# The first layer and the last step of a convolution filter as four 64-row, 64-column TensorE tiles

## The chip, the cores and the metric

The kernel runs on one core of a Trainium2 chip. The metric is the time of one execution on the device, in microseconds (us). The engines are named as in the profile: PE (TensorE; PEld are its weight loads), DVE (VectorE), ACT (ScalarE), POOL (GpSimd) and SP, whose queue issues most transfers.

## The reference

Two stages follow each other: a gated long convolution over each of four sequences, whose filter comes from a small two-layer network, and a soft mixture of eight experts over all 45,824 tokens. The change lies in the filter, the first lines:

```
h_mlp = np.maximum(pos_emb @ w1, 0.0) @ w2          # (11456, 64) @ (64, 64), then @ (64, 128)
window = np.exp(-0.01 * pos)[:, None]
h_filt = h_mlp * window
u = x * v
y = irfft(rfft(u, 2S) * rfft(h_filt, 2S))[:, :S]     # S = 11456, per channel
out = x * y                                          # then the mixture of experts
```

## The kernel before, in words

The transforms are done as matrix products over a two-step factorization with N1 = 111 and N2 = 197: a position is 111 j + r with j below J = 99 and r up to 55 in either direction, so R = 56 values of r. The 128 channels go in G = 8 groups of 16. All products are fp32; each stands in the trace as two matmul instructions, each with its own weight load.

The filter comes first. `hid_load` brings `pos_emb` in 14 tiles `pos` (four r each): partitions 0 to 63 hold the 64 features of the positions 111 j + r, partitions 64 to 127 those of 111 j - r. `w1s` is `w1` as a block-diagonal 128 x 128 table (made on the host by `_twice`), so that one product with the tile gives the 64 outputs of both directions side by side. The window's factor in r is `wins`; since it is positive it is put into the weights ahead of the ReLU: `w1r[:, r]` is `w1s` times one column of `wins`. `hid_scale` makes these, some one at a time on DVE or ACT (`scale_one`), the rest several at a time on POOL (`scale_many`).

`hid_step` handles 4, then five times 8, then 4, 4, 2 and 2 values of r: one product per r (L161), then ACT applies ReLU to the first half (`hb`, L164), and DVE, twice, forms the second half's ReLU plus and minus `hb` (L166) and writes the hidden tensor `hid`. `idle_products` are products of zeros (L125), eight at the start, three after the first step and four at the end.

Then `filter_first` (L207) and `filter_second` (L219) transform `hid` over j and r into `F`. Group 0 of the signal goes through its first transform (`first`, L185, four tiles of 64 x 64 at `tile_position` (0 or 64, 0 or 64)); DVE has by then made its inputs (`p1_sd`). Last, in 13 rounds, `filter_last` multiplies eight frequencies of `F` by `w2` (L229: two tiles, each of 64 rows and 111 columns of weights), ACT copies the result into `ring`, and `p2` (L356 and after) forms the spectrum products of the same eight frequencies on PE, DVE and POOL. The seven other groups, the inverse transforms and the experts follow.

The order on each engine is that of the program text: `inorder` records every instruction, and `hid_scale` runs three steps ahead of `hid_step`. SP issues `wins`, the `pos` tiles, then the signal's `x` and `v` tiles and the tables, in that order.

Of the kernel before, what the change touches and what calls it, by code (L numbers as in the profile page):

```python
# [11 lines left out]
F32 = mybir.dt.float32  # L12
F32R = mybir.dt.float32r
AF = mybir.ActivationFunctionType
ALU = mybir.AluOpType
# [4 lines left out]
N1, N2 = 111, 197  # L20
L = N1 * N2
J = 99
# [3 lines left out]
R = 56  # L26
RP = 64
FO = 64
# [20 lines left out]
@with_exitstack  # L49
def conv_gate_moe(ctx: ExitStack, tc: tile.TileContext, xf, vf, xi, xe, pos, w1, w2, win,  # L50
                  t1x, t1h, wt, t3, t4, phi, mw1, mw2, rep, out):
    nc = tc.nc
    dram = ctx.enter_context(tc.tile_pool(name="dram", bufs=1, space=bass.MemoryType.DRAM))
    hs = dram.tile([G - 1, HP, J, 2 * CG], F32, tag="hs", name="hs")
    scr = dram.tile([D * TOK], F32, tag="scr", name="scr")
    cp = ctx.enter_context(tc.tile_pool(name="cp", bufs=1))
    moe = Moe(tc, cp, scr, phi, mw1, mw2, rep, out)
    with ExitStack() as cctx:
        conv_part(cctx, tc, cp, moe, xf, vf, xi, xe, pos, w1, w2, win, t1x, t1h, wt, t3, t4, hs, scr)
    moe.run(ctx)  # L60


def conv_part(ctx, tc, cp, moe, xf, vf, xi, xe, pos, w1, w2, win, t1x, t1h, wt, t3, t4, hs, scr):
    nc = tc.nc
# [3 lines left out]
    psh = hid_ps.enter_context(tc.tile_pool(name="psh", bufs=4, space=bass.MemoryType.PSUM))  # L68
# [9 lines left out]
    Tall = cp.tile([128, (B + 1) * 2 * CG * J], F32, tag="T", name="T")  # L78
# [4 lines left out]
    inorder = tc.keep_in_program_order  # L83

    RB = 4
# [6 lines left out]
    hid = moe.E[:J, : 2 * RP * FO].rearrange("p (s r f) -> p s r f", s=2, r=RP)  # L92
    Tf = T.rearrange("p s b c k i -> p (s b c) k i")
    Th = Tall[:, : J * 2 * FO].rearrange("p (k x) -> p k x", k=J)
    F = moe.E[:, : J * N1].rearrange("p (k n) -> p k n", n=N1)
# [1 line left out]
    ring = moe.E[:, J * N1 : J * N1 + 2 * HK * 2 * D]  # L97
    ring = ring.rearrange("p (t g k x) -> p t g k x", t=2, g=G, k=HK)
    small = moe.E[:, J * N1 + 2 * HK * 2 * D :]
    w1s = small[:, : 2 * FO]  # L100
    w2s = small[:, 2 * FO : 2 * FO + D]
    wins = small[:, 2 * FO + D :][:, :R]
    tab1h = small[:J, 2 * FO + D + R :][:, : 4 * J]
    w1r = Tall[:, : R * 2 * FO].rearrange("p (r x) -> p r x", r=R)
    spare = [moe.E[:, 4 * C * R + PW * i :][:, :PW] for i in range(2)]

    def hid_load(i):
# [9 lines left out]
    HR = 8  # L117
    sizes = [RB] + [HR] * 5 + [RB, RB, 2, 2]
    steps = [(sum(sizes[:i]), n) for i, n in enumerate(sizes)]
    zero = hid[:, 0, R : R + 2].rearrange("p r f -> p (r f)")  # L120
# [3 lines left out]
        for _ in range(n):  # L124
            inorder(nc.tensor.matmul(t, lhsT=zero, rhs=zero, start=True, stop=True))  # L125

    def scale_one(eng, r):
        if eng is nc.scalar:
            inorder(eng.activation(w1r[:, r], w1s, AF.Copy, scale=wins[:, r : r + 1]))
        else:  # L130
            inorder(eng.tensor_scalar_mul(w1r[:, r], w1s, wins[:, r : r + 1]))

    def scale_many(r0, r1):
        inorder(nc.gpsimd.tensor_tensor(
            out=w1r[:, r0:r1], in0=w1s.unsqueeze(1).to_broadcast([128, r1 - r0, 2 * FO]), op=ALU.mult,
            in1=wins[:, r0:r1].unsqueeze(2).to_broadcast([128, r1 - r0, 2 * FO])))

    def hid_scale(i):
        r0, n = steps[i]
        if i == 0:  # L140
            for r in range(1, n):
                scale_one(nc.vector, r)
        elif i == 1:
            for r in range(r0, r0 + 4):
                scale_one(nc.scalar, r)
            scale_many(r0 + 4, r0 + n)
        else:
            if n == HR:
                for r in range(r0 + n - 2, r0 + n):
                    scale_one(nc.scalar, r)  # L150
                n -= 2
            if n == 2:
                scale_one(nc.scalar, r0 + 1)
                n = 1
            scale_many(r0, r0 + n)

    def hid_step(r0, n):
        ph = psh.tile([J, HR, 2, FO], F32, tag="ph", name=f"ph_{r0}")
        for k in range(n):
            r = r0 + k  # L160
            inorder(nc.tensor.matmul(ph[:, k].rearrange("p h f -> p (h f)"), lhsT=pts[r // RB][:, r % RB],  # L161
                                     rhs=w1r[:, r] if r else w1s, start=True, stop=True))
        hb = ld.tile([J, HR, FO], F32, tag="lv", name=f"hb_{r0}", bufs=2)
        inorder(nc.scalar.activation(hb[:, :n], ph[:, :n, 0], AF.Relu))  # L164
        for s, op in enumerate((ALU.add, ALU.subtract)):
            inorder(nc.vector.scalar_tensor_tensor(out=hid[:, s, r0 : r0 + n], in0=ph[:, :n, 1], scalar=0.0,  # L166
                                                   op0=ALU.max, op1=op, in1=hb[:, :n]))

    def banks(g, u, name, large):
# [7 lines left out]
    def first(g, u, sd, large=False):  # L177

        ps = [t[:, : 4 * J].rearrange("p (c s k) -> p c s k", c=2, s=2) for t in banks(g, u, "p1", large)]
        for i in range(2):  # L180
            for s in range(2):
                for h in range(2):
                    js = slice(RP * h, RP * h + JH)
                    for d in range(2):
                        inorder(nc.tensor.matmul(  # L185
                            ps[h][RP * d : RP * d + RP, i, s, :], lhsT=sd[js, i, s, d, :],
                            rhs=tab1x[js, J * (s + d) : J * (s + d + 1)],
                            start=True, stop=True, tile_position=(RP * h, RP * d)))
        return ps
# [33 lines left out]
    def filter_last(k):  # L223

        n = min(4, J - k)
        ps = [psb.tile([N1, 4, G, CG], F32, tag="psb", name=f"fl{s}_{k}") for s in range(2)]
        for i in range(n):
            for s in range(2):
                inorder(nc.tensor.matmul(ps[s][:, i].rearrange("p g c -> p (g c)"),  # L229
                                         lhsT=F[FO * s : FO * s + FO, k + i, :],  # L230
                                         rhs=w2s[FO * s : FO * s + FO],
                                         start=True, stop=True, tile_position=(FO * s, 0)))
        for s in range(2):
            dst = ring[:N1, k // HK % 2, :, k % HK : k % HK + n, CG * s : CG * s + CG]
            inorder(nc.scalar.activation(dst, ps[s][:, :n].rearrange("p k g c -> p g k c"), AF.Copy))  # L235
        if k % HK or k + 4 >= J:
            k0 = k // HK * HK
            n = min(HK, J - k0)
            nc.sync.dma_start(out=hs[:, :, k0 : k0 + n, :].rearrange("g p k x -> p g (k x)"),
                              in_=ring[:HP, k0 // HK % 2, 1:, :n].rearrange("p g k x -> p g (k x)"))  # L240
# [45 lines left out]
                                      op=op))  # L286
        return sd

    nc.scalar.dma_start(out=w1s, in_=w1)
    inorder(nc.vector.memset(zero, 0.0))  # L290
    inorder(nc.gpsimd.memset(hid[:, 0, R + 2 : RP], 0.0))
    inorder(nc.gpsimd.memset(hid[:, 1, R:RP], 0.0))
    idle_products(8)
    pts = {}
    nc.gpsimd.dma_start(out=w2s, in_=w2)
    inorder(nc.sync.dma_start(out=wins, in_=win))
    for i in range(12):
        hid_load(i)
    for i in range(3):
        hid_scale(i)  # L300
    for i, (r0, n) in enumerate(steps):
        hid_step(r0, n)
        if i == 0:
            idle_products(3)
        for k in range(r0 // RB, (r0 + n) // RB):
            if k + 12 < NS:
                hid_load(k + 12)
        if i + 3 < len(steps):
            hid_scale(i + 3)
        if i == 2:  # L310
            inorder(nc.sync.dma_start(out=tab1h, in_=t1h))
# [176 lines left out]
    for g in range(G + 1):  # L488
# [6 lines left out]
        elif g < G:  # L495
# [21 lines left out]
            ps = [first(g, u, sds[u], not large) for u in range(2)]  # L517
# [54 lines left out]
        if g == 0:  # L572
            sds = next_sds
            for i, k in enumerate(ks):
                if k % HK == 0:
                    for w in range(k, min(J, k + HK), 4):
                        filter_last(w)
                p2(g, k)
                if i in (1, 5, 9, 13):
                    u = PRE + i // 4  # L580
                    sds[u] = p1_sd(1, u, nc.vector)
            continue
# [521 lines left out]
    return dict(rep=rep, t1x=t1x, t1h=t1h, wt=wt, t3=t3, t4=t4, win=win)  # L1104


def _twice(a):
    o = np.zeros((2, a.shape[0], 2, a.shape[1]), a.dtype)
    o[0, :, 0] = o[1, :, 1] = a
    return o.reshape(2 * a.shape[0], -1)  # L1110


def _index(base):
    j = np.arange(-(JT // 2), JT // 2 + 1) if base else np.arange(J)
    r = np.arange(R)
    p = N1 * j[:, None] + r[None] + base
    b = N1 * j[:, None] - r[None] + base
    m = -N1 * j[:, None] - r[None] + base
    return p, b, m
# [99 lines left out]
```

## Time and profile before

| | us |
|---|---|
| median of three runs | 902.09 (901.45 to 903.24) |
| the profiled execution | 902.57 |
| its span in the trace | 900.8 |
| PE busy (matmul) | 866.0, 96% |
| PE weight loads | 794.9, 88% |
| DVE busy | 723.2, 80% |
| ACT busy | 455.4, 51% |
| POOL busy | 386.5, 43% |

All times inside the kernel are counted from the start of the span. A row of the trace has a line of the kernel (L161 is line 161), an engine, an operation, the tiles that it writes and reads, and a count; what stands behind an arrow ended the idle time before it. "Issue" means that the engine waited for nothing that the profile shows. PEclk is the clock that TensorE was granted, as a share of the full clock.

### The profile page before, as it was taken

To read this page: it belongs to the slowest core of one execution; us is meant where nothing else is said; L and a number is where in the kernel's file an instruction comes from. 1 tells how busy PE (TensorE), PEld (TensorE's weight loads), DVE (VectorE), ACT (ScalarE), POOL (GpSimd) and SP (SyncE) were. 2 spreads that over 40 slices of the span, in tenths; PEclk is the share of its full clock that TensorE was granted. 3 is DMA by queue.
4 is the path that set the end of the run, shared out by engine and by line. 5 is a ranking of instruction groups with operands and counts; after the bars stand their busy time and mean duration, and the time that the engine had idled before them with its cause. 6 is when DMAs were issued, how large, how long until landed. Compare 5 with 4: busy or idle time off the path is not lost.

```text
span 900.8 us, 37252 instructions
## 1 busy us (share of the span) xinstructions
PE 866.0 (96%) x16190; PEld 794.9 (88%) x16190; DVE 723.2 (80%) x1242; ACT 455.4 (51%) x968; POOL 386.5 (43%) x526
## 2 busy tenths in 40 slices
PE   9999999999999999999999999999999988999992
PEld 9998989999999999999999999999999975666441
DVE  6967966898899889979988997998796178974682
ACT  5775557316612831581185148217613547986662
POOL 5003850591096039208803940690194005644950
PEclk9999999999999999999999999999999999999996
DMA  9964675548647655863675577467436998971698
GB/s 313 396 198 133 207 231 166 170 116 276 192 131 220 210 165 162 262 205 123 206 233 162 147 245 224 152 176 244 140 77 209 354 298 315 313 269 66 263 417 365
DMA packets 95170, 197.02 MB, mean 219 GB/s; under 512 B 14345, under 2 KB 57259, under 8 KB 91166
## 3 DMA queue, kind: packets, MB, share of 16 engines
q1 hardware_dynamic: 94830, 194.50, 66.0%
q8 instruction: 128, 2.10, 0.9%
q14 instruction: 36, 0.29, 0.1%
q10 hardware_dynamic: 144, 0.07, 0.0%
q0 software_dynamic: 32, 0.07, 0.0%
HBM read 137.73 MB, written 56.86 MB: 216 GB/s over the span
## 4 chain that ended last, share of the span: by engine, by line
PE 87%; DVE 5%; ACT 2%; POOL 2%; DMA 2%; issue 1%; DVEq 0%; ACTq 0%; SPq 0%; POOLq 0%
PE p L376 22%; PE p L356 20%; PE p L426 17%; PE p L185 10%; PE pw L1052 3%; PE fl L229 3%; PE f L207 2%; PE f L219 2%; PE ph L161 1%; PE pa L852 1%; PE ct L899 1%; PE pt L697 1%; PE pl L771 1%; ACT et L816 1%; DMA xreg<-scr 1%
## 5 line engine op out<-in xcount | busy, mean ns | idle before, releaser
L366 POOL TENSOR_TENSOR T<-m 111x256 f32<-111x256 f32 (+1 forms) x199 | 151.0, 759 | 344.4 <-DVE m L360 344.3
L360 DVE TENSOR_TENSOR m<-p,T 111x1024 f32<-111x1024 f32 (+1 forms) x175 | 200.2, 1203 | 13.0 <-PE p L356 6.4
L376 PE MATMUL p<-tab,T 111*99 111x112 f32 x2048 | 205.3, 260 | 1.8 <-ACT T L197 0.3
L376 PEld LDWEIGHTS p<-tab,T 111*99 111x99 f32 x2048 | 198.9, 170 | 6.7 <-issue 1.8
L356 PE MATMUL p<-T,W 128*64 128x128 f32 (+1 forms) x3168 | 196.5, 276 | 0.2 <-DVE m L360 0.2
L435 ACT ACTIVATE vc<-p 128x416 f32<-128x416 f32 x112 | 51.8, 515 | 267.9 <-PE p L426 228.3
L356 PEld LDWEIGHTS p<-T,W 128*64 128x64 f32 (+1 forms) x3168 | 181.5, 127 | 2.4 <-DVE m L360 0.7
L426 PE MATMUL p<-tab,E 99*64 99x104 f32 x3584 | 173.5, 252 | 1.1 <-DVE E L389 0.6
L426 PEld LDWEIGHTS p<-tab,E 99*64 99x64 f32 x3584 | 166.2, 136 | 2.2 <-DVE E L389 0.7
L391 ACT ACTIVATE E<-p 99x448 f32<-99x448 f32 x254 | 131.9, 576 | 64.4 <-PE p L376 58.3
L367 POOL TENSOR_TENSOR T<-m 111x256 f32<-111x256 f32 (+1 forms) x199 | 147.5, 741 | 0.0
L197 ACT ACTIVATE T<-p 128x396 f32<-128x396 f32 x240 | 100.3, 539 | 11.0 <-PE p L185 10.9
L185 PE MATMUL p<-tab1x,x 53*64 53x99 f32 x3648 | 86.9, 246 | 1.2 <-issue 1.0
L185 PEld LDWEIGHTS p<-tab1x,x 53*64 53x64 f32 x3648 | 79.8, 132 | 5.6 <-issue 1.2
L448 DVE TENSOR_TENSOR p<-p,vc 128x832 f32<-128x832 f32 x49 | 50.2, 1024 | 11.4 <-ACT vc L435 11.4
L824 POOL TENSOR_TENSOR E<-lt,mx 128x1024 f32<-128x1024 f32 (+2 forms) x12 | 21.6, 1798 | 81.1 <-DVE mx L823 81.1
L279 DVE TENSOR_TENSOR x<-x,T 128x448 f32<-128x448 f32 x51 | 31.5, 618 | 22.2 <-DMA x<-in_xf_dram 15.2
L456 DVE TENSOR_TENSOR E<-p,E 128x824 f32<-128x824 f32 x39 | 39.6, 1016 | 1.3
L285 DVE TENSOR_TENSOR x<-T 128x224 f32<-128x224 f32 x102 | 39.2, 425 | 1.8
L281 DVE TENSOR_TENSOR T<-x 128x224 f32<-128x224 f32 x102 | 39.2, 425 | 1.7
L703 ACT ACTIVATE xreg<-pt 128x512 f32<-128x512 f32 (+1 forms) x70 | 36.0, 615 | 4.9 <-PE pt L697 4.8
L235 ACT ACTIVATE E<-fl 111x512 f32<-111x512 f32 (+1 forms) x50 | 26.8, 627 | 21.3 <-PE fl L229 21.3
(135 smaller groups left out, 982.4 us busy)
## 6 DMA issues: line engine op xcount, KB each, us to landing
x<-in_xf_dram SPq DMA_DIRECT2D x114, 256.0 KB, 4.3
out_dram<-xreg SPq DMA_DIRECT2D x16, 1024.0 KB, 6.5
E<-in_xi_dram SPq DMA_DIRECT2D x39, 412.0 KB, 4.1
T<-in_vf_dram SPq DMA_DIRECT2D x65, 224.0 KB, 5.0
scr<-E SPq DMA_DIRECT2D x70, 206.0 KB, 3.9
T<-hs SPq DMA_DIRECT2D x63, 154.0 KB, 4.4
hs<-E SPq DMA_DIRECT2D x12, 784.0 KB, 4.6
mv<-in_vf_dram SPq DMA_DIRECT2D x42, 224.0 KB, 4.6
```

What stands on the lines that cost most here:

```text
L185: inorder(nc.tensor.matmul(ps[h][RP * d : RP * d + RP, i, s, :], lhsT=sd[js, i, s, d, :], rhs=tab1x[js, J * (s + d) : J * (s + d + 1)], st ...
L197: inorder(nc.scalar.activation(dst, src, AF.Copy))
L356: inorder(nc.tensor.matmul(ps[ns, i].rearrange("p b c -> p (b c)"), lhsT=W[:, k0 + i, ns], rhs=Tf[:, :, k0 + i, :], start=True, stop=True, ...
L360: inorder(nc.vector.tensor_mul(m[:, :n].rearrange("p k s e c i -> p k s (e c i)").rearrange("p k s (b c) -> p k s b c", c=CG), ps[:, :n].u ...
L366: inorder(eng.tensor_tensor(out=Ty[:, 0], in0=m[:, :n, 0, 0], in1=m[:, :n, 1, 1], op=ALU.subtract))
L367: inorder(eng.tensor_tensor(out=Ty[:, 1], in0=m[:, :n, 1, 0], in1=m[:, :n, 0, 1], op=ALU.add))
L376: inorder(nc.tensor.matmul(pk[:, i, 2 * s : 2 * s + 2, :].rearrange("p q r -> p (q r)"), lhsT=T[0:N1, s, 2 * k + i, u // 2, :, u % 2], rhs ...
L391: inorder(nc.scalar.activation(dst, src, AF.Copy))
L426: inorder(nc.tensor.matmul(pv[RP * h : RP * h + RP, 2 * k + i, w, :], lhsT=E[:J, r, 2 - 2 * w + s, :], rhs=tab4[:, s, o : o + NJ], start=( ...
L435: inorder(nc.scalar.activation(vc[:, w], pv[:, :, 0, :], AF.Copy, scale=2.0 * w - 1.0))
L448: inorder(nc.vector.tensor_tensor(out=pw, in0=pw[:, 1:2].to_broadcast([128, 2, 4, NJ]), in1=vc, op=ALU.add))
L456: inorder(nc.vector.tensor_mul(xw, pw[:, :, :, 1:], xw))
```

## The change

The block-diagonal `w1` goes: `w1s` is now `w1` twice, one copy in each half of the partitions, and `w1r[:, r]` has 64 columns instead of 128. Each product of the first layer becomes four: the two directions (signs of r) in the two halves of the array's rows, the tokens j in two column tiles of 64 and 35. The output tile `pt` has the two directions in different banks. The last filter step is cut the same way in its output: the 111 rows become tiles of 64 and 47, so four tiles instead of two. All single scalings go to ACT; `win` is loaded by ACT's queue behind `w1` instead of by SP ahead of `pos`; ACT gets a small activation on zeros ahead of its first scaling. Lines after L130 are renumbered by a few: the first layer's product is L162, the last step's L235.

ACT at its start, before (`T` holds `w1r`, `E` holds `w1s` and `wins`, `ph` the products of a step, `hb` their ReLU):

```order
L289 DMA E<-in_w_dram 128x128
L129 ACT_TABLE_LOAD
L129 ACTIVATE T<-E 128x128 x6
L164 ACTIVATE hb_129<-ph_124 99x256
L129 ACTIVATE T<-E 128x128 x2
L164 ACTIVATE hb_151<-ph_142 99x512
```

The same place on ACT now:

```order
L294 DMA E<-in_w_dram 128x64
L295 DMA E<-in_win_dram 128x56
L297 ACT_TABLE_LOAD
L297 ACTIVATE E<-E 99x2
L128 ACTIVATE T<-E 128x64 x9
L167 ACTIVATE hb_142<-ph_125 99x256
L128 ACTIVATE T<-E 128x64 x2
```

The load of `win` has come to this queue, the table load stands ahead of the scalings behind an activation of its own, and nine scalings of half the width stand where six were.

PE in the first layer's first two steps, before (`pos` are the loaded tiles; a wait's name is the engine or queue waited for):

```order
L161 MATMUL ph_124<-E,pos_92 99x128 [waits DMAHW2_49,DMAHW0_49]
L161 MATMUL ph_124<-T,pos_92 99x128 [waits DVE_49] x3
L125 MATMUL idle<-E 128x128 x3
L161 MATMUL ph_142<-T,pos_94 99x128 [waits DMAHW3_49,Activation_49]
L161 MATMUL ph_142<-T,pos_94 99x128 [waits Activation_49] x3
```

PE over the end of the first step and the first product of the second one now:

```order
L162 MATMUL ph_125<-T,pos_93 64x64 [waits Activation_49]
L162 MATMUL ph_125<-T,pos_93 35x64
L125 MATMUL idle<-E 128x128 x3
L162 MATMUL ph_155<-T,pos_95 64x64 [waits DMAHW3_49,Activation_49]
L162 MATMUL ph_155<-T,pos_95 35x64
```

Where one product stood per r, four stand now, 64 and 35 rows in turn, and those of the first step wait for ACT where they waited for DVE.

On SP nothing is changed but that the load of `win` at the head of the queue is gone and the first `pos` tile stands there. The diff's core:

```
-    w1s = small[:, : 2 * FO]
+    w1s = small[:, :FO]
...
-    w1r = Tall[:, : R * 2 * FO].rearrange("p (r x) -> p r x", r=R)
+    w1r = Tall[:, : R * FO].rearrange("p (r x) -> p r x", r=R)
...
-    def scale_one(eng, r):
-        if eng is nc.scalar:
-            inorder(eng.activation(w1r[:, r], w1s, AF.Copy, scale=wins[:, r : r + 1]))
-        else:
-            inorder(eng.tensor_scalar_mul(w1r[:, r], w1s, wins[:, r : r + 1]))
+    def scale_one(r):
+        inorder(nc.scalar.activation(w1r[:, r], w1s, AF.Copy, scale=wins[:, r : r + 1]))
...
     def hid_step(r0, n):
-        ph = psh.tile([J, HR, 2, FO], F32, tag="ph", name=f"ph_{r0}")
+        pt = psh.tile([128, 2, HR, FO], F32, tag="ph", name=f"ph_{r0}")
         for k in range(n):
             r = r0 + k
-            inorder(nc.tensor.matmul(ph[:, k].rearrange("p h f -> p (h f)"), lhsT=pts[r // RB][:, r % RB],
-                                     rhs=w1r[:, r] if r else w1s, start=True, stop=True))
+            for h in range(2):
+                fs = slice(FO * h, FO * h + FO)
+                for c in range(2):
+                    js = slice(RP * c, min(RP * c + RP, J))
+                    inorder(nc.tensor.matmul(pt[js, h, k], lhsT=pts[r // RB][fs, r % RB, js],
+                                             rhs=w1r[fs, r] if r else w1s[fs], start=True, stop=True,
+                                             tile_position=(FO * h, RP * c)))
+        ph = pt[:J]
...
         for i in range(n):
             for s in range(2):
-                inorder(nc.tensor.matmul(ps[s][:, i].rearrange("p g c -> p (g c)"),
-                                         lhsT=F[FO * s : FO * s + FO, k + i, :],
-                                         rhs=w2s[FO * s : FO * s + FO],
-                                         start=True, stop=True, tile_position=(FO * s, 0)))
+                fs = slice(FO * s, FO * s + FO)
+                for h in range(2):
+                    ns = slice(RP * h, min(RP * h + RP, N1))
+                    inorder(nc.tensor.matmul(ps[s][ns, i].rearrange("p g c -> p (g c)"), lhsT=F[fs, k + i, ns],
+                                             rhs=w2s[fs], start=True, stop=True,
+                                             tile_position=(FO * s, RP * h)))
...
-    nc.scalar.dma_start(out=w1s, in_=w1)
+    inorder(nc.scalar.dma_start(out=w1s, in_=w1))
+    inorder(nc.scalar.dma_start(out=wins, in_=win))
     inorder(nc.vector.memset(zero, 0.0))
+    inorder(nc.scalar.activation(small[:J, FO : FO + 2], zero[:, :2], AF.Relu))
...
-    inorder(nc.sync.dma_start(out=wins, in_=win))
```

## Rows read from the trace of the kernel before

**Rows 1.** Chain of waits, 0 to 140 us: start, length, what.
```profile
6.72 11.55 PE ph L161 x104
...
19.60 22.21 PE f L207 x254
...
61.67 7.22 PE p L185 x302
...
75.15 1.93 PE fl L229 x32
77.08 1.97 PE p L356 x31
```

**Rows 2.** Waits, 60 to 140 us: total, times, longest.
```profile
DVE T L199 <- PE p L185: 8.6, 4, 5.9
```

**Rows 3.** Timeline, 0 to 20 us: start, length, instructions [idle before].
```profile
2.73 1.28 ACT L129 ACT_TABLE_LOAD   x1 [2.73 <-DMA E<-in_win_dram]
2.84 2.70 DVE L131 TENSOR_SCALAR T<-E 128x128 f32<-128x128 f32 x3 [1.83 <-DMA E<-in_w_dram]
...
4.03 1.86 ACT L129 ACTIVATE T<-E 128x128 f32<-128x128 f32 x6
...
6.50 0.76 DVE L166 SCALAR_TENSOR_TENSOR E<-ph,hb 99x256 f32<-99x256 f32 x2 [0.97 <-ACT hb L164]
6.56 11.70 PE L161 MATMUL ph<-T,pos 128*99 128x128 f32 x104
8.51 0.60 ACT L164 ACTIVATE hb<-ph 99x512 f32<-99x512 f32 x1 [1.46 <-PE ph L161]
...
9.14 1.29 DVE L166 SCALAR_TENSOR_TENSOR E<-ph,hb 99x512 f32<-99x512 f32 x2 [1.88 <-ACT hb L164]
...
16.17 3.52 DVE L166 SCALAR_TENSOR_TENSOR E<-ph,hb 99x512 f32<-99x512 f32 x10 [0.46 <-ACT hb L164]
```

**Rows 4.** Timeline of PE's weight loads, 60 to 76 us.
```profile
65.92 1.49 PEld L185 LDWEIGHTS p<-tab1x,E 53*64 53x64 f32 x67 [0.19 <-issue]
...
69.92 0.14 PEld L185 LDWEIGHTS p<-tab1x,x 53*64 53x64 f32 x3 [1.23 <-issue]
...
73.38 1.58 PEld L185 LDWEIGHTS p<-tab1x,mv 53*64 53x64 f32 x70 [0.68 <-issue]
```

**Rows 5.** Windows: busy and instructions of PE, PEld, DVE, ACT, POOL; PEclk, DMA share, GB/s.
```profile
13.22:65.91 52.69, 51.88 (x891) 50.75 (x889) 43.22 (x109) 35.81 (x70) 0.00 (x0) 1.00 0.89 320
65.91:69.92 4.01, 2.98 (x129) 2.78 (x128) 2.30 (x5) 2.00 (x4) 0.00 (x0) 1.00 0.06 15
69.92:73.37 3.45, 2.97 (x128) 2.78 (x128) 2.28 (x4) 2.00 (x4) 0.00 (x0) 1.00 0.48 144
...
794.79:801.93 7.14, 6.16 (x131) 4.18 (x130) 5.76 (x11) 6.13 (x15) 3.13 (x3) 1.00 0.87 297
735.76:739.17 3.41, 1.53 (x24) 0.72 (x26) 2.20 (x7) 0.49 (x1) 0.00 (x0) 1.00 0.92 305
739.17:742.58 3.41, 3.20 (x44) 2.53 (x44) 2.35 (x7) 3.15 (x7) 0.57 (x1) 0.50 1.04 377
5.30:8.70 3.40, 3.40 (x32) 3.38 (x32) 0.99 (x3) 1.75 (x7) 3.40 (x4) 1.00 1.02 345
```

**Rows 6.** The page's DMA queues: packets, MB, share of 16 engines.
```profile
q8 instruction: 128, 2.10, 0.9%
```

**Rows 7.** DMA queues, 69.92 to 71.02 us (all), then 71.0 to 72.1.
```profile
q1 hardware_dynamic: 123, 0.22, 52.6%
...
q8 instruction: 1, 0.02, 5.7%
```

**Rows 8.** DMA queues, 13.22 to 15.75 us (all), then 15.75 to 17.0.
```profile
q1 hardware_dynamic: 566, 0.96, 106.6%
...
q8 instruction: 1, 0.02, 5.6%
```

**Rows 9.** Timeline of PE's matmuls, 794 to 806 us.
```profile
801.93 0.72 PE L697 MATMUL pt<-aux,xreg 64*128 64x64 f32 x17 [0.99 <-issue]
```

More of the change, by code (lines that the diff above doesn't have):

```diff
@@ L125, in idle_products @@
             inorder(nc.tensor.matmul(t, lhsT=zero, rhs=zero, start=True, stop=True))
-    def scale_one(eng, r):
-        if eng is nc.scalar:
-            inorder(eng.activation(w1r[:, r], w1s, AF.Copy, scale=wins[:, r : r + 1]))
-        else:
-            inorder(eng.tensor_scalar_mul(w1r[:, r], w1s, wins[:, r : r + 1]))
+    def scale_one(r):
+        inorder(nc.scalar.activation(w1r[:, r], w1s, AF.Copy, scale=wins[:, r : r + 1]))
     def scale_many(r0, r1):
         inorder(nc.gpsimd.tensor_tensor(
-            out=w1r[:, r0:r1], in0=w1s.unsqueeze(1).to_broadcast([128, r1 - r0, 2 * FO]), op=ALU.mult,
-            in1=wins[:, r0:r1].unsqueeze(2).to_broadcast([128, r1 - r0, 2 * FO])))
+            out=w1r[:, r0:r1], in0=w1s.unsqueeze(1).to_broadcast([128, r1 - r0, FO]), op=ALU.mult,
+            in1=wins[:, r0:r1].unsqueeze(2).to_broadcast([128, r1 - r0, FO])))
     def hid_scale(i):
@@ L141, in hid_scale @@
             for r in range(1, n):
-                scale_one(nc.vector, r)
+                scale_one(r)
         elif i == 1:
             for r in range(r0, r0 + 4):
-                scale_one(nc.scalar, r)
+                scale_one(r)
             scale_many(r0 + 4, r0 + n)
@@ L149, in hid_scale @@
                 for r in range(r0 + n - 2, r0 + n):
-                    scale_one(nc.scalar, r)
+                    scale_one(r)
                 n -= 2
             if n == 2:
-                scale_one(nc.scalar, r0 + 1)
+                scale_one(r0 + 1)
                 n = 1
@@ L157, in hid_step @@
     def hid_step(r0, n):
-        ph = psh.tile([J, HR, 2, FO], F32, tag="ph", name=f"ph_{r0}")
+        pt = psh.tile([128, 2, HR, FO], F32, tag="ph", name=f"ph_{r0}")
         for k in range(n):
             r = r0 + k
-            inorder(nc.tensor.matmul(ph[:, k].rearrange("p h f -> p (h f)"), lhsT=pts[r // RB][:, r % RB],
-                                     rhs=w1r[:, r] if r else w1s, start=True, stop=True))
+            for h in range(2):
[6 more added lines that the diff above has]
+        ph = pt[:J]
         hb = ld.tile([J, HR, FO], F32, tag="lv", name=f"hb_{r0}", bufs=2)
-        inorder(nc.scalar.activation(hb[:, :n], ph[:, :n, 0], AF.Relu))
+        inorder(nc.scalar.activation(hb[:, :n], ph[:, 0, :n], AF.Relu))
         for s, op in enumerate((ALU.add, ALU.subtract)):
-            inorder(nc.vector.scalar_tensor_tensor(out=hid[:, s, r0 : r0 + n], in0=ph[:, :n, 1], scalar=0.0,
+            inorder(nc.vector.scalar_tensor_tensor(out=hid[:, s, r0 : r0 + n], in0=ph[:, 1, :n], scalar=0.0,
                                                    op0=ALU.max, op1=op, in1=hb[:, :n]))
@@ L1104, in _constants @@
     return dict(rep=rep, t1x=t1x, t1h=t1h, wt=wt, t3=t3, t4=t4, win=win)
[L1107 to L1110, printed above, removed]
 def _index(base):
@@ L1198 @@
     k = _constants()
-    feeds = dict(xf=xf, vf=vf, xi=xi, xe=xe, pos=pe, w1=_twice(inputs["w1"]), w2=np.concatenate([inputs["w2"], inputs["w2"]], 0), win=k["win"],
+    feeds = dict(xf=xf, vf=vf, xi=xi, xe=xe, pos=pe, w1=np.concatenate([inputs["w1"], inputs["w1"]], 0), w2=np.concatenate([inputs["w2"], inputs["w2"]], 0), win=k["win"],
                  t1x=k["t1x"], t1h=k["t1h"], wt=k["wt"], t3=k["t3"], t4=k["t4"],
```

## The prediction

> **What bounds the kernel now.** I read the chain of waits first, over the filter part (0 to 140 us) where every edit lies. It is PE almost without a break [rows 1]: the first layer (L161), four idle products, `filter_first` (L207) from 19.60 us, `filter_second` (L219), the first transform of group 0 (L185) from 61.67, then 13 rounds in which the last filter step (L229) and the spectrum products (L356) take turns, 1.93 and 1.97 us. A microsecond by which `filter_first` starts earlier or later should therefore reach the end. There is slack on the other side: DVE has its part of L185 ready 5.9 us before L185 delivers [rows 2].
>
> Then the timeline of the first 20 us [rows 3]. From 6.56 us PE works through L161 at its own pace, 104 instructions in 11.70 us. DVE (two instructions a step) waits for ACT's `hb`, which waits for PE. So PE sets the pace, and a faster first layer looks like a gain. What speaks against it is how PE gets its instructions.
>
> **A limit on the instruction stream.** In L185, the stage that has four tiles already, PE's weight loads break off before 65.92, 69.92 and 73.38 us, each time released by "issue": PE waited for nothing that the profile shows [rows 4]. Between the breaks PE took 129 matmuls and 128 loads, then 128 and 128 [rows 5]: 256 instructions from break to break (one matmul lies over an edge). The queue called "instruction" brings 2.10 MB in 128 packets over the whole span [rows 6], 16.4 KB each; PE has 2 x 16190 instructions, 253 a packet. So PE's program comes in blocks of 256. After the break that ended at 69.92 no packet starts before 71.02, one does by 72.1 [rows 7], and PE goes on at 73.38. A block is 2.97 us of PE work there, yet blocks took 4.01 and 3.45 us [rows 5], with DMA at 0.06 and 0.48.
>
> Under load it is worse. From 794.79 to 801.93 us, DMA at 0.87, a block took 7.14 us [rows 5], and its end is again a wait for "issue", 0.99 us before L697 [rows 9]. Counting seven blocks back from 65.91 (891 + 889 instructions in that window and 12 semaphore waits) puts a block's edge at 13.22 us [rows 5]. Its packet is not in the window up to 15.75 us and is in the next [rows 8]: 2.5 us behind the edge instead of 1.1, with DMA full. I call c the time from a block's first instruction to the next block's when PE has run dry; one block is always ahead.
>
> [...]
>
> **First layer.** Before: 56 products of two matmul instructions, 112 with 112 loads. After: four products for each, 448 with 448. The price per matmul lies between 23.2 ns (2.97 us for 128 at 99 columns [rows 5]) and 15.0 ns if it goes with columns (64/99). I take 15, so 0.12 us for each of 56 rows and 6.7 us in all where it was 12.3; at 23.2 it would be 10.4, still under the price of the stream. For 896 instructions are 3.5 blocks. Up to the edge now at 13.22 us PE has run 44 instructions of idle products and about 145 of L161, after the change 145/16 = 9 rows. The next edges come every 16 rows: at 25, at 41, and past 56 inside the last idle products.
>
> When are these edges passed? The first step starts at 4.6 us as now, the second at 6.3, row 9 is reached at 6.9 and row 25 at 8.8. For c the rows give 3.45 at the lowest and 7.14 at the highest. The stretch 5.3 to 8.7 us carries 345 GB/s at a DMA share of 1.02 [rows 5], nearer to the loaded rows; 3.6 plus the 1.4 us by which the packet after 13.22 came later than on idle queues gives c = 5.0. For the first edge I take 4.5, as PE is not dry yet. So row 25 goes on at 11.4, row 41 at 16.4, and the block of `filter_first` at 21.4 us. DVE would be done sooner: 0.4 us for the rest of the step of row 41, 0.60 for `hb`, 3.52 for DVE's last five steps [rows 3], 20.9. With 0.1 us of hand-over `filter_first` starts at 21.5 instead of 19.60: **+1.9 us**. Ends: c = 3.45 gives row 41 at 13.5 and, by DVE, a start at 18.1 (-1.5); c = 7.14 gives 27.9 (+8.3). It costs from c = 4.3 on.
>
> **Scalings.** DVE's three (2.70 us from 2.84) go to ACT. DVE gains nothing, as its next work at 6.50 waits for `hb` [rows 3]. ACT has nine of 64 columns where it had six of 128: at 0.31 us as now (1.86 for six) 2.8 us, less if columns count. Its table load, which now waits 2.73 us for `win`, goes ahead of that wait. `win` is issued behind `w1` on ACT's queue, 0.4 us later, and lands at about 3.1. So ACT is free at 5.9 us, as now; without the early table load it would be 1.3 later, which the stall before row 25 would hide. SP loses one issue, so the `pos` loads start 0.4 us earlier: no gain, L161 does not wait for them once it runs. POOL's products halve in size and run ahead of their use: zero. The smaller `w1` load, the warm-up activation and the changed bank layout: zero, under PE's idle products up to 4.6 us.
>
> **TensorE's clock.** New idle time of some 3 us stands three times in the stage. [...] If `filter_first` begins at half clock, one such stretch costs 1.7 us. I take half of it, **+0.9**, with 0 and +3.4 (two stretches) as ends.
>
> **First transform of group 0.** Unchanged, but 672 more instructions (2.6 blocks) move its edges to 214, 470, 726 and 982 of its 1024, from 118, 374, 630 and 886. With 3.7 us a block (mean of 4.01 and 3.45) it takes 2.3 + 3.1 + 3.7 + 3.7 + 0.5 = 13.3 instead of 13.5 (61.67 to 75.15 [rows 1]): **-0.2**, between -0.8 and +0.5.
>
> **Last filter step.** Twice the instructions, half the output rows each. A group of tiles streams 128 columns as before: 32 matmuls in 1.93 us now; four tiles, by L185's 128 in 2.97 us, half of that times 128/99: 1.92. What a change of form costs between the two lines is not separate in these rows; 0.05 us a round either way is 0.6 over 13 rounds. I take **0.0**, with -0.6 and +0.6. A round becomes 192 instructions in 3.9 us, a block 4.9 to 5.2 us, above c on idle queues; that is its cover, and if c is 5.0 here too, some 10 blocks lose 0.1 us each, +1.
>
> **Sum.** The profiled execution took 902.57 us, 0.48 over the median 902.09. 902.57 + 1.9 + 0.9 - 0.2 + 0.0 = 905.2; on the median's scale **904.7 us**. A measurement of this kernel can tell about 0.2% (1.8 us) from no change.
>
> **Rivals.**
> (1) No change to speak of: the stream is limited as on idle queues, c of 3.5 to 4.2. `filter_first` starts at 18.1 to 19.5, the clock costs 0 to 0.9: 900.4 to 902.7. For it: 3.45 and 4.01 are the rows with the same four-tile form. Against: DMA is full here and was not there. 25%.
> (2) Faster: the stream does not bind, instructions come as fast as 15 ns a pair. Then DVE sets the stage: its second step begins at 6.3 + 0.96 + 0.60 = 7.9 us, four steps of 1.29 and then 3.52 end at 16.6, `filter_first` at 16.8, -2.8; PE's pauses are short, so nothing for the clock; -0.2 in L185: 899.1 us. It decides where a block comes within 2.7 us. For it: L161 never broke off before. Against: it then spent 14 us on a block (11.70/208 x 256). 15%.
> (3) The loaded price in full, c = 7.14: +8.3 and +0.9, 911 us. Against: that stretch also holds waits for data. 8%.
> (4) The change does not do what it says, the four tiles run one after another: 448 matmuls of 60 ns, 27 us. L185's 23 ns speak against it; not counted.
>
> **How the numbers follow.** The forecast, c of 4.3 to 6.0, has 52% and its own range is 902 to 908. The range of 8 in 10 takes in rival 1 and the clock's upper end, and leaves out rival 2 and rival 3: 900.0 to 909.0. Faster by over 0.2%: rival 2 and a little of rival 1, 0.16. Within 0.2%: most of rival 1 and the low end of the forecast, 0.34. Slower: 0.50.
>
> **What would show it.** Right: in the first 22 us PE's new first layer (L162) breaks off about every 256 instructions, near rows 25 and 41, released by "issue", with an instruction packet shortly before each restart; ACT and DVE wait for PE; `filter_first` starts between 20 and 23 us; PE's later stages keep their lengths but for L185. Wrong: L162 without such breaks and DVE back to back (rival 2), breaks under 1.5 us (rival 1), a clock of 1.00 throughout, or a round of the last step and L356 more than 0.1 us off 3.90, which would put the change of time elsewhere.

## The result

The changed kernel takes 907.55 us (median of 6 runs, 906.24 to 908.77). The kernel before took 902.49 us beside it (6 runs, 900.77 to 903.49). The ratio is 1.0069, with an interval of 1.0051 to 1.0088: slower by 5 us, where 904.7 us and a range of 900 to 909 had been predicted. The profiled execution of the changed kernel took 906.24 us with a span of 904.5 us, against a span of 900.8 before.

The chain of waits of the changed kernel, first 80 us (start, length, what), is what answers to [rows 1]. L162 is the first layer (L161 before), L210 `filter_first` (L207), L222 `filter_second` (L219), L188 the first transform (L185), L169 DVE's part of the first layer (L166).

```profile
6.63 2.60 PE ph L162 x161
9.23 2.98 issue
12.21 3.63 PE ph L162 x125
15.84 1.39 issue
17.24 0.65 PE ph L162 x27
...
18.59 1.96 DVE E L169 x4
...
21.03 1.81 issue
22.84 1.67 PE idle L125 x7
...
24.56 24.32 PE f L210 x255
...
49.47 19.24 PE f L222 x376
68.70 8.02 PE p L188 x359
76.72 0.35 issue
```

The first layer itself became fast: 161 matmul instructions in 2.60 us, 16 ns each. Three times after that PE has nothing to do and waits for nothing that the profile shows: "issue", for 2.98, 1.39 and 1.81 us. In the trace an instruction packet starts at 9.51, 14.73 and 20.44 us, 2.4 to 2.7 us ahead of each restart (12.21, 17.24 and 22.84 us); this is the sign that the prediction had asked for. The second of them, in the queues from 14.6 to 16.0 us (from 12.21 to 14.6 us there is none):

```profile
q8 instruction: 1, 0.02, 5.0%
```

`filter_first` starts at 24.56 us; it started at 19.60 [rows 1]. It is also longer, 24.32 us instead of 22.21. From there on the two kernels run in parallel: `filter_second` starts 7.07 us later than before (42.40 to 49.47 us), and L188, which is a little shorter, hands on at 81.75 us what L185 handed on at 75.15, 6.60 us later. The next rows are the windows of the changed kernel over the block from its first edge to the first restart, over its two full blocks of instructions, over three stretches that the granted clock divides, and over a piece of `filter_first`; columns as in [rows 5].

```profile
7.13:12.21 5.08, 2.10 (x144) 1.96 (x133) 2.99 (x6) 2.25 (x7) 2.67 (x6) 1.00 1.07 328
12.21:17.24 5.03, 3.63 (x127) 3.46 (x128) 2.58 (x4) 1.19 (x2) 0.00 (x0) 0.66 1.05 366
17.24:22.84 5.60, 2.74 (x124) 2.35 (x124) 4.19 (x12) 2.28 (x7) 0.00 (x0) 0.97 1.04 382
...
12.31:15.73 3.42, 3.42 (x126) 3.35 (x127) 1.48 (x3) 1.19 (x2) 0.00 (x0) 0.50 1.04 360
15.73:22.55 6.82, 2.86 (x128) 2.35 (x124) 5.03 (x13) 2.28 (x7) 0.00 (x0) 1.00 1.04 381
22.55:29.38 6.83, 6.48 (x37) 4.98 (x38) 6.57 (x18) 1.54 (x3) 0.00 (x0) 0.50 1.03 385
...
25.40:28.80 3.40, 3.40 (x24) 2.52 (x22) 3.29 (x9) 1.03 (x2) 0.00 (x0) 0.50 1.03 368
```

Between two breaks PE took 127 matmuls and 128 loads: again blocks of 256. One took 5.03 us and the next 5.60 us, with DMA at 1.05 and 1.04. The work of a block is 2.10 us at the full clock (first row); the rest of its 5.08 us is waiting. The granted clock is 0.50 from 12.31 to 15.73 us, behind the first pause, and again from 22.55 to 29.38 us, from within the third pause; `filter_first` begins in this second stretch. The last row is all `filter_first`, 24 matmuls in 3.40 us.

So most of the loss is made by 25 us, and the rest while `filter_first` runs at the lower clock. What is left of it at the end is 3.7 us in this pair of profiles and 5 us in the medians.

### The profile page after: what moved, and what is told of

It reads as the page before. It is cut to its first block, busy times and chain, and to the rows that moved or that the text cites. A ratio compares the mean times of both kernels' runs of the same rounds, so it can differ in the third digit from the quotient of the medians.

```text
span 904.5 us, 38716 instructions
## 1 busy us (share of the span) xinstructions
PE 863.9 (96%) x16922; PEld 790.6 (87%) x16922; DVE 721.2 (80%) x1239; ACT 456.1 (50%) x972; POOL 382.8 (42%) x526
## 4 chain that ended last, share of the span: by engine, by line
PE 88%; DVE 5%; POOL 2%; ACT 2%; issue 2%; DVEq 0%; ACTq 0%; POOLq 0%
PE p L382 22%; PE p L362 20%; PE p L432 17%; PE p L188 10%; PE pw L1058 3%; PE f L210 3%; PE fl L235 3%; PE f L222 2%; PE pa L858 1%; PE pl L777 1%; PE pt L703 1%; PE ct L905 1%; ACT et L822 1%; PE ph L162 1%; DVE lt L790 1%
## 5 line engine op out<-in xcount | busy, mean ns | idle before, releaser
L188 PE MATMUL p<-tab1x,x 53*64 53x99 f32 x3648 | 86.7, 246 | 0.2 <-ACT E L240 0.2
L188 PEld LDWEIGHTS p<-tab1x,x 53*64 53x64 f32 x3648 | 79.8, 132 | 4.4 <-ACT E L240 0.4
L284 DVE TENSOR_TENSOR x<-x,T 128x448 f32<-128x448 f32 x51 | 31.6, 619 | 21.4 <-DMA x<-in_xf_dram 9.8
L1058 PE MATMUL pw<-cs,so 32*128 32x512 f32 (+3 forms) x192 | 34.8, 633 | 3.1 <-DVE xreg L1065 1.9
```

Of the source, the lines that this page charges most:

```text
L188: inorder(nc.tensor.matmul(ps[h][RP * d : RP * d + RP, i, s, :], lhsT=sd[js, i, s, d, :], rhs=tab1x[js, J * (s + d) : J * (s + d + 1)], st ...
L1058: inorder(nc.tensor.matmul(po[:, :na].rearrange("p k t -> p (k t)"), lhsT=so[NSLOT * a : NSLOT * a + NSLOT], rhs=ct[NSLOT * a : NSLOT * a ...
```

## The experiments

Each kernel ran beside runs of the kernel before on the same chip; ratios are against those.

**One part alone: the last filter step.** The kernel before with only this edit:

```
-            inorder(nc.tensor.matmul(ps[s][:, i]..., lhsT=F[FO * s : FO * s + FO, k + i, :], ... tile_position=(FO * s, 0)))
+            for h in range(2):
+                ... matmul(ps[s][ns, i]..., lhsT=F[fs, k + i, ns], ... tile_position=(FO * s, RP * h))
```

> Only the last filter step in four tiles; first layer, scalings and loads as before. Theory (the stream of instructions is what costs, in the first layer): PE's first layer stays at 11.7 us with no break, filter_first starts at 19.6, a round of the last step and the spectrum products takes 3.87 us instead of 3.90, and the time is 902.1, within 0.8 of before. Rival (the last step's doubled stream costs its part later on): over 904.

Measured: 902.2 us (12 runs) against 901.94; ratio 1.0008, 0.9988 to 1.0028. No change. Its chain of waits shows the rounds (L232 is the last step, L358 the spectrum products):

```profile
83.07 1.90 PE fl L232 x62
84.97 1.97 PE p L358 x31
```

Twice the instructions take 1.90 us where 32 took 1.93 [rows 1]. A round is 3.87 us instead of 3.90, and a block of 256 instructions is then 5.2 us of PE's work (3.87 x 256/192). In the chain up to 90 us the rounds have one wait by "issue", 0.73 us in the first (79.94 us). `filter_first`, expected at 19.6 us, starts at 22.65 in this profile, for a reason that lies ahead of the edit (last section).

**The other part alone: the first layer and the scalings.** The changed kernel with that loop put back to two tiles:

```
-                for h in range(2):
-                    ... matmul(ps[s][ns, i]..., lhsT=F[fs, k + i, ns], ... tile_position=(FO * s, RP * h))
+                inorder(nc.tensor.matmul(ps[s][:, i]..., lhsT=F[FO * s : FO * s + FO, k + i, :], ... tile_position=(FO * s, 0)))
```

> The first layer in four tiles with all that belongs to it, the last step as before. Theory: breaks at rows 25, 41 and behind the first idle product, filter_first at about 24.5, 907.9 us: all of the loss, and 0.4 more than with the last step changed too. Rival (the last step is what loses): under 904.

Measured: 909.2 us (6 runs), ratio 1.0088, 1.0066 to 1.011. The whole loss is in the first layer with its scalings. The chain has the three waits again, though `filter_first` starts at 22.83 us and not at the 24.5 expected: the blocks come about 1 us earlier in this profile. Of that, 0.7 us goes back, since `filter_first` takes 25.04 us here and 24.32 in the changed kernel.

```profile
9.12 2.14 issue
...
14.30 1.96 issue
...
20.48 1.18 issue
21.66 1.12 PE idle L125 x7
...
22.83 7.18 PE f L210 x46
```

**The scalings alone.** The kernel before with all small products on ACT, `win` on ACT's queue and the early activation, but `w1` 128 columns wide and the first layer as it was:

```
-                scale_one(nc.vector, r)
+                scale_one(nc.scalar, r)
...
+    inorder(nc.scalar.dma_start(out=wins, in_=win))
...
-    inorder(nc.sync.dma_start(out=wins, in_=win))
```

> The kernel before with only the scalings moved: all small products of w1 on ACT, win issued by ACT behind w1, the activation ahead of it; w1 stays 128 columns wide and the first layer has its old products. Theory (PE sets the pace of the first layer and neither ACT nor POOL is waited for once it runs): within 0.5 us of the kernel before, 902 to 903. Rival (win lands 1.2 us later than by SP's queue, ACT ends its nine scalings and POOL starts 1.2 us later, and the first layer starts its second step that much later): filter_first 0.5 to 1.2 us later, 903 to 904.

Measured: 901.04 us (10 runs), ratio 0.9992, 0.9977 to 1.0008: no change, though `win` lands later. The timeline of the changed kernel on ACT shows that delay:

```profile
4.33 2.26 ACT L128 ACTIVATE T<-E 128x64 f32<-128x64 f32 x9 [1.16 <-DMA E<-in_win_dram]
```

My working had `win` at 3.1 us, and it came at 4.3. That costs nothing: the second step of the first layer started at 6.56 us in both kernels, the one before and the changed one, since the nine scalings take 2.26 us instead of the 2.8 that I had put down.

So the loss belongs to the four tiles in the first layer. The next runs ask what in them.

**Half the instructions.** The changed kernel with its first layer in two row tiles, 448 instructions instead of 896:

```
-                for c in range(2):
-                    inorder(nc.tensor.matmul(pt[js, h, k], lhsT=pts[r // RB][fs, r % RB, js], ... tile_position=(FO * h, RP * c)))
+                inorder(nc.tensor.matmul(pt[:J, h, k], lhsT=pts[r // RB][fs, r % RB, :], ... tile_position=(FO * h, 0)))
```

> As the changed kernel, but the first layer in two tiles (both directions in row tiles, all 99 tokens in one column tile of 99): the same columns streamed, half the instructions, 448 instead of 896. Theory: the blocks' edges fall at rows 18 and 50; the block behind row 50 is asked for at about 8 us and is there at about 13, when PE arrives; DVE sets the pace, filter_first starts at 17.0 (16.5 to 18.0), 899.5 us, faster than before. Rival (the narrow tiles, the scalings on ACT or the new order of loads lose the time): filter_first stays after 21 and the time over 905.

Measured: 912.69 us (6 runs), ratio 1.0119, 1.0099 to 1.014. The expected gain did not come, and I had the wrong reason in view. PE's timeline (start, length, instructions, idle time ahead) has no break by "issue" any more, but the first layer (L160) is slow by itself:

```profile
6.30 1.65 PE L125 MATMUL idle<-E 99*128 99x128 f32 x6
7.88 17.60 PE L160 MATMUL ph<-T,pos 64*99 64x64 f32 x208
25.41 2.07 PE L125 MATMUL idle<-E 99*128 99x128 f32 x8
27.54 24.20 PE L208 MATMUL f<-E 99*64 99x198 f32 x256
```

A matmul instruction takes 85 ns. The eight instructions of idle products behind it take 2.07 us, where they took 1.13 us in the kernel before (18.27 us) at a granted 1.00; in the changed kernel seven took 1.67 us (22.84 us) at a granted 0.50. By that pace TensorE is at the lower clock here, and I take it to have been so throughout the layer. The windows of this run show when that ends:

```profile
28.74:32.15 3.41, 3.41 (x24) 2.52 (x22) 3.27 (x10) 1.32 (x3) 0.00 (x0) 1.00 0.82 244
32.15:35.56 3.41, 3.41 (x42) 3.37 (x42) 3.31 (x9) 2.44 (x6) 0.00 (x0) 1.00 1.04 372
```

24 matmuls in 3.41 us, then 42, with PE busy throughout in both. The 1.00 of the first row cannot be taken at its word: this run has no record of the clock before 32.15 us, and the same products of the changed kernel at a recorded 0.50 are as slow (25.40 to 28.80 us, above). So the breaks are gone, but at this pace a block holds 10.8 us of work (128 x 85 ns), and no break would be seen with any of the prices above: the run is no test of the stream, and what the first layer would cost in this form at the full clock it does not say.

**The same, with full products ahead.** The same kernel with nine idle products behind the first step where it had three, to raise the clock:

```
-            idle_products(3)
+            idle_products(9)
```

> The run with two row tiles (half the instructions of four tiles), with nine idle products behind the first step where it had three, so that TensorE has full products up to the second step. Theory (the granted clock was the whole loss of the two row tiles; once it is 1.00 it stays): no breaks by issue, the first layer at about half the time it took, DVE sets the pace, filter_first at about 18 us (1.2 us go for the added products), 901 to 902. Rival (two row tiles by themselves let the clock fall): the clock is 1.00 around 6 to 8 us and 0.50 again within the first layer, filter_first after 24 us, 910 to 914.

Measured: 913.91 us (2 runs), ratio 1.0132, 1.0094 to 1.017. Neither theory holds: by PE's pace the clock did not rise at 6 to 8 us and fall again, nor at any time before the first layer was over.

```profile
6.31 4.21 PE L125 MATMUL idle<-E 99*128 99x128 f32 x18
10.45 17.60 PE L160 MATMUL ph<-T,pos 64*99 64x64 f32 x208
```

Eighteen instructions of idle products at 234 ns each are the pace of the lower clock (239 ns each in the changed kernel at a granted 0.50, 141 ns in the kernel before at 1.00), and the first layer takes 17.60 us once more. What two row tiles cost at the full clock, these two runs cannot tell.

**The same instructions, less on the DMA queues.** The changed kernel, with SP's loads of `x` and `v` (and all that stands behind them) held until DVE has ended the first layer:

```
+        if g == 0 and u == 0:
+            inorder(nc.vector.memset(xt[:, 0, 0, :2], 0.0))
```

> As the changed kernel, but the first x tile's load waits for DVE's end of the first layer (a write of DVE on that tile), so that SP's queue is empty while the first layer runs on; the time as a whole must suffer, since the loads come some 10 us later. Theory (the block's price grows with the load on DMA): the block behind row 41 and the one after it take 3.5 to 4.0 us from edge to edge instead of 5.0 and 5.6, and filter_first starts at 20.5 to 21.5 instead of 24.6. Rival (the price is the same under any load): 5.0 and 5.6 as in the changed kernel.

PE's instructions and their blocks are those of the changed kernel. The windows over its blocks, over the stretch of lower clock and over `filter_first`:

```profile
12.31:16.22 3.91, 3.54 (x126) 3.38 (x127) 1.96 (x4) 1.19 (x2) 0.00 (x0) 0.56 0.04 9
16.22:19.90 3.68, 2.62 (x124) 2.31 (x124) 2.94 (x8) 1.98 (x6) 0.00 (x0) 1.00 0.02 4
12.50:15.92 3.42, 3.35 (x126) 3.19 (x120) 1.66 (x3) 1.19 (x2) 0.00 (x0) 0.50 0.03 8
21.01:43.20 22.19, 22.19 (x256) 21.87 (x256) 16.21 (x43) 16.24 (x31) 0.00 (x0) 1.00 0.93 336
```

With DMA at 0.04 and 0.02 the blocks take 3.91 and 3.68 us, not 5.03 and 5.60; the first one, 5.11 us up to 12.31 us and still beside the `pos` loads (a DMA share of 0.89), is as long as in the changed kernel. `filter_first` starts at 21.01 us, at the full clock, and takes 22.19 us as in the kernel before. This is the run that settles the cause: the same products in the same tiles on PE; what has changed is the traffic beside the fetches (and one small write on DVE), and the pauses shrink with it. The instruction packets say how: in the changed kernel they start 2.5 and 3.2 us behind the blocks' edges (14.73 and 20.44 us), here 1.2 and 1.3 us (13.51 and 17.55 us), while the packets themselves take 1.0 to 1.4 us in both. Beside full queues the fetch started later; why it did is not shown. It was one execution of 903.24 us, so it was timed again:

> The run with the loads of x and v held until DVE has ended the first layer, once more and timed in rounds. Theory (the price of a block of instructions hangs on what DMA moves beside it; held loads lower it from over 5 to under 4 us, and the clock then stays up for filter_first, at the price of x and v coming some 10 us late): between the kernel before and the changed kernel, 903 to 905, ratio 1.001 to 1.003. Rival (the single time of 903.24 was one from the lower end, and the late loads cost what the blocks gain): 907, as the changed kernel, ratio 1.005 or more.

Measured: 906.54 us (10 runs) against 903.04; ratio 1.0041, 1.0019 to 1.0062. That lies between the two kernels and above what I had given; by time alone it is not apart from the changed kernel. The trace says where the gain goes. The first of the two blocks takes 4.13 us; the second, 3.92 us, is nearly all PE's own work at the lower clock (3.81 us), with no pause behind it. `filter_first` starts at 21.29 and `filter_second` at 44.07 us, 5.4 us ahead of the changed kernel. But the `x` and `v` come late: L188 begins at 63.22 us, breaks off, waits for DVE and hands on at 80.16 us, only 1.6 us ahead of the changed kernel:

```profile
11.95 3.00 PE L162 MATMUL ph<-T,pos 64*35 64x64 f32 x126 [2.52 <-issue]
16.08 3.81 PE L162 MATMUL ph<-T,pos 64*64 64x64 f32 x123 [1.13 <-issue]
...
21.29 22.19 PE L210 MATMUL f<-E 99*64 99x198 f32 x256 [0.20 <-PE idle L125]
```

```profile
69.05 0.97 DVE T L202 x2
70.02 0.04 issue
70.06 8.90 PE p L188 x324
...
PE p L188 <- DVE T L202: 1.8, 1, 1.8
```

The first rows are its timeline, the next its chain of waits, and the last is from its list of waits (total, times, longest): DVE's own work stands in the chain up to 70 us. In the kernel before DVE was 5.9 us early there [rows 2]. Holding the loads is therefore a test and no remedy.

**Without the idle products behind the first layer.**

```
-    idle_products(4)
```

> The changed kernel without the four idle products behind the first layer. In the changed kernel the third edge of a block lies inside these products: all but the first of them wait for the block (22.84 us) and then run 1.67 us at half clock ahead of filter_first, which starts at 24.56. Theory (the block's arrival plus these products set the start): filter_first has nearly all its instructions in the block that comes at 22.8, starts its bulk at 22.9, 1.7 us earlier, and the time falls to about 905.8. Rival (the products hold the clock up, and without them filter_first and filter_second run longer at half clock): filter_first starts earlier by 1.7 but gives it back by 30 us, 907 to 908.

Measured: 909.39 us (4 runs), ratio 1.0079, 1.0052 to 1.0105. No gain.

```profile
17.09 3.92 PE L162 MATMUL ph<-T,pos 64*64 64x64 f32 x123 [1.94 <-issue]
22.25 0.60 PE L210 MATMUL f<-E 99*64 99x198 f32 x1 [1.25 <-DVE E L169]
23.11 23.59 PE L210 MATMUL f<-E 99*64 99x198 f32 x255 [0.27 <-issue]
```

`filter_first` does start its bulk 1.45 us earlier, at 23.11. `filter_second` follows at 47.30 instead of 49.47, and this execution is still 1.9 us ahead of the changed kernel's at the last filter step (79.88 against 81.75 us), at the end no longer (spans of 904.7 and 904.5). Behind the filter part profiles differ without an edit there (below), and with 4 runs between 906.44 and 911.2 a gain of that size is not excluded. Neither theory is settled by it.

**A form that stays under the stream.** The kernel before with only the steps of rows 4 to 11 and 20 to 27 in four tiles, 192 instructions more instead of 672:

```
+    TILED = (4, 20)
...
+            if not tiled:
+                inorder(nc.tensor.matmul(pt[:J, 2 * FO * k : 2 * FO * k + 2 * FO], lhsT=pts[r // RB][:, r % RB],
+                                         rhs=rhs, start=True, stop=True))
+                continue
+            for h in range(2):
+                for c in range(2):
+                    inorder(nc.tensor.matmul(ph[js, h, k], ..., rhs=rhs[fs, fs], ..., tile_position=(FO * h, RP * c)))
```

> The kernel before with only the steps of rows 4 to 11 and 20 to 27 in four tiles, all others as one full product a row; scalings and the last filter step as before. 192 instructions more instead of 672: the first edge of a block falls at about 9.3 us inside the fourth step, the second behind the first layer. Theory (the loss of the changed kernel is the instruction stream, so a form that stays under a block in 5 us keeps the gain in PE's time, 16 rows by 0.095 us): no break by issue in the first layer, filter_first at about 18.1 us instead of 19.6, 900.6, a ratio of 0.998 to 0.999. Rival (the four-tile form costs by itself, in hand-over or in clock): filter_first at 19.6 or later, 902 or more.

Measured: 901.61 us (12 runs) against 902.14; ratio 1.0013, 0.999 to 1.0036. Its timeline on PE (L177 four tiles, L170 full products):

```profile
6.62 1.15 PE L177 MATMUL ph<-T,pos 64*64 64x64 f32 x64
7.71 1.99 PE L170 MATMUL ph<-T,pos 128*99 128x128 f32 x16
9.63 1.15 PE L177 MATMUL ph<-T,pos 64*64 64x64 f32 x64
10.71 6.54 PE L170 MATMUL ph<-T,pos 128*99 128x128 f32 x56
17.26 1.13 PE L125 MATMUL idle<-E 99*128 99x128 f32 x8
18.59 21.69 PE L224 MATMUL f<-E 99*64 99x198 f32 x253 [0.20 <-PE idle L125]
```

There is no break, the four tiles do their steps in 1.15 us where eight rows of the old form take 1.8 (11.70/52 x 8 [rows 3]), and `filter_first` starts at 18.59, 1.01 us earlier, where 1.5 had been expected. So in these two steps four tiles cost nothing by themselves. The microsecond is below what 12 runs can tell: the time is that of the kernel before. I found no version that is measurably faster than both.

## Why the prediction was right, and where its sizes were off

The direction and the mechanism held: the stream of instructions sets the first layer's pace (pauses of 2.98, 1.39 and 1.81 us), the granted clock falls to 0.50 behind the first of these pauses and within the third (from 12.31 and 22.55 us), and the other three edits do nothing that shows in the time. The predicted difference was 2.6 us and the medians give 5.1. By the steps:

**The edges.** Predicted near rows 25 and 41 and inside the last idle products; they lie there. The restarts were given as 11.4, 16.4 and 21.4 us and came at 12.21, 17.24 and 22.84. I had put the first block at 4.5 us and the others at c = 5.0. They took 5.1 (from PE's reaching the first edge, some 7.1 us), 5.03 and 5.60. Of the 1.4 us by which the third restart was missed, 0.8 lie in the first block (0.2 of it because PE reached its edge later than the 6.9 that I had put down) and 0.6 in the third. The GB/s do not order the three prices: 328, 366 and 382 here, 345 in the stretch I had read c from [rows 5]; what sets c more finely is open. By the steps of the working, the lower end (c = 3.45) gives a start at 17.9 us and not at 18.1; nothing else hangs on it.

**The step that failed** is the one behind the third edge. I had put that edge "inside the last idle products", and then let `filter_first` start with the block's arrival. Of the eight instructions of these products seven lie behind the edge (`22.84 1.67 PE idle L125 x7` in the chain), and they go first, at the lower clock. That is 1.7 us, which stood in no term. With the 1.4 us above it makes 24.6 out of 21.5; 24.56 was measured. The term of the start, +1.9, measured +4.96.

DVE was not far from being the bound instead. It ran its last five steps from 18.59 without a break:

```profile
18.59 3.53 DVE L169 SCALAR_TENSOR_TENSOR E<-ph,hb 99x512 f32<-99x512 f32 x10 [1.76 <-ACT hb L167]
```

That is the timeline of the changed kernel on DVE: done at 22.12, 0.7 us before the block came.

**The clock.** Predicted +0.9 with ends of 0 and 3.4. The 0.9 is half of the 1.7 us that I had put down for one stretch of 3.41 us at a granted 0.50, such as the one from 739.17 us [rows 5]. No run shows that term; it was an estimate. In its place the runs showed a longer stretch: `filter_first` took 24.32 us instead of 22.21, +2.1, and it began in the stretch from 22.55 to 29.38 us, which was granted at 0.50 and of which 4.8 us lie behind its start. The first dip, 12.31 to 15.73, cost nothing, since PE was done with that block at 15.84 and waited for the next until 17.24. The run with the held loads is the cross-check: the same products, clock at 1.00, 22.19 us.

**The first transform.** Predicted -0.2; 68.70 to 81.75 is 13.05 us, 13.48 before: -0.4. Its two breaks lie at 76.72 and 80.04 us (0.35 and 0.96 us), and from the one restart to the other it is 3.93 us, where it was 4.01 and 3.45 before [rows 5].

**The last filter step.** Predicted 0.0 with 0.6 either way; 1.90 instead of 1.93 us a round, 13 x 0.03 = -0.4, and nothing in the time of the run with this part alone.

**The sum.** 4.96 + 2.1 - 0.4 - 0.4 = 6.3 us at the end of the filter part. The trace shows 6.6 us at 81.75 us, before the last step's 0.4. It is still 7.0 us where the mixture of experts begins (L697, now L703, starts at 741.23 instead of 734.23 us), and 3.7 at the end, in this pair of profiles. The mixture has no edit, so what comes back there is no effect of the change that I could show. Set against this profile of the kernel before, eight of the ten other profiles (the changed kernel's too) win back 2 to 4 us in the mixture, the one with the scalings alone among them (+1.6 at its start, -1.1 at the end, though its own `filter_first` came 1.3 us late, at 20.91), which points to time that the profile of the kernel before lost there. That the forecast time came within 3 us is therefore in part luck: in the profiles the filter part lost 6.6 us where 2.6 had been forecast.

**The rivals.** The stream limited as on idle queues (25%) is what the kernel with held loads shows, 3.7 to 4.1 us a block: the price is right, but it is not paid under the traffic of this stage. That the stream does not bind (15%) is refuted by the breaks. The loaded price in full, 7.14 us (8%), was too high: 5.0 to 5.6. The tiles one after another, at 60 ns a matmul (not counted), are refuted by 16 ns.

How much of a block's price is seen went with the work in the block. With over 5 us of PE's work in it, in the last filter step alone (up to 90 us) and in the run with two tiled steps (up to `filter_first`), the one wait is that of 0.73 us; with 2.1 us there were 2.98 us of waiting at the first such boundary.

## What to carry to other kernels

Count instructions beside columns: here tiles that run side by side made 896 instructions out of 224, and the stage was then as fast as its blocks of 256 arrived. That was 3.5 to 4.1 us a block beside quiet DMA queues (shares of 0.01 to 0.48) and 5.0 to 5.6 us beside loads that fill them (0.89 to 1.07), so work that was packed to 2.1 us a block gained nothing and got pauses in return. Where an edge of a block fell inside filler work, the filler behind it (1.67 us) moved with the edge and stood ahead of the next stage. And a pause had a second price in the clock of what came after it: the granted 0.50 from 22.55 us on, within the third pause, made `filter_first` 2.1 us longer.

## What was not expected of the hardware

- **The block's price hung on the traffic beside it.** The same blocks took 5.03 and 5.60 us at a DMA share of 1.05 and 1.04, and with the loads held 3.91 and 3.68 us at 0.04 and 0.02. The packet took no longer beside full queues (1.0 to 1.4 us in both); it started later behind the edge, by 2.5 and 3.2 us against 1.2 and 1.3.
- **Two row tiles ran at the pace of the lower clock.** PE was busy without a break, and yet the first layer in this form took 85 ns a matmul instruction from start to end, in two profiles, one of them with 4.2 us of full products ahead. In both the pace rose only after the stage, in the first from 24 matmuls in 3.41 us to 42 at 32.15 us, in the second not before 35 us. In the kernel before and the changed one the first record of the clock, 1.00, begins at 5.30 and 5.49 us. Why is open.
- **When the clock first rises differs from run to run.** The kernel with only the last step changed has the same PE work as the kernel before up to there; its timeline:

```profile
6.90 0.75 PE L161 MATMUL ph<-T,pos 128*99 128x128 f32 x2 [0.68 <-DVE T L131]
7.44 1.49 PE L125 MATMUL idle<-E 99*128 99x128 f32 x6
8.72 12.58 PE L161 MATMUL ph<-T,pos 128*99 128x128 f32 x104
```

The six instructions of idle products took 1.49 us; in the kernel before, in its own profile, they took 0.83 us, and the clock's first record begins at 10.52 us here and at 5.30 there. Not all of it is the clock: PE also waited 0.68 us for DVE, whose three scalings took 4.04 us and not 2.70 [rows 3]. The run with the scalings alone has no such wait, the same 1.49 us, and its first record at 7.96 us. The execution above reached `filter_first` 3.05 us later, at 22.65, and took 907.54 us, while the median of the same kernel is 902.2. So a single profile of this kernel can be off by 3 us at the start of `filter_first` alone, and this one was 5 us off at the end, as much as the change itself costs. The profiles with breaks (the changed kernel, its first layer alone, the held loads twice, the one without the idle products) are not of that kind: there the six instructions took 0.94 to 1.00 us, and the second step started between 6.45 and 6.76 us, at 6.56 in the kernel before.
